# Weights behind the first inputs, first steps on their own, and mixture pieces carried over a block's end

## The chip, the cores and the metric

One core of one Trainium2 chip. The metric is the device time of one execution in microseconds (us), the span of that core. The kernel before has a median of 1416.5 us in three runs. The engines are PE (TensorE matmul), DVE (VectorE), ACT (ScalarE), POOL (GpSimd) and SP (SyncE, which issues most transfers).

## The reference, cut to what matters

An RWKV-7 attention (batch 4, 8 heads, 768 steps, head size 40) feeds a dense mixture of four experts (3072 rows of 320, hidden size 1024).

```python
for t in range(S):                      # attention, per batch and head
    y[:, :, t] = einsum('bhd,bhde->bhe', rt, state)
    Sa = einsum('bhde,bhe->bhd', state, at)
    state = state * wt[:, :, None, :] - einsum('bhd,bhe->bhde', Sa, bt) + einsum('bhd,bhe->bhde', vt, kt)
# ... rows (B*S, H*D) ...
p = domain_probs / (domain_probs.sum(-1, keepdims=True) + 1e-09)
for e in range(E):                      # mixture
    h = np.maximum(x @ w1[e], 0.0)
    out += p[:, e:e + 1] * (h @ w2[e])
```

## The kernel before

The 768 steps are cut into 12 chunks of 64, done in seven blocks: block zero has one chunk, blocks one to five have two each, block six has one. For each block the attention goes through four stages.

- **Units** (two per chunk). Each unit's inputs natW, natNK, natKN, natA, natR are loaded, transposed on PE (pW, pNK, ...), scaled, and multiplied to triangles (pef). The triangles go through HBM (FD) into the tile Gl. There is one tile of each nat kind, so a unit's load waits until the unit before has been transposed.
- **Solve**: one long chain of DVE instructions on Gl, about 30 us.
- The solution goes through HBM to F and XT, and PE works on it (pi, px).
- **Steps**: the recurrence, then a gather into xT for the mixture.

The mixture of block y runs on PE among the attention of block y+1, as a queue of pieces. Each of the four experts has four *wide* pieces (ph: 20 matmuls in a block of two chunks, then a relu on ACT), then four *narrow* ones (po: 16 matmuls, then an *eviction*, which scales po by the gate and writes it to osb; on DVE). `mix(us)` gives out so many us of pieces at that place of the program:

```python
def bank(name):                                    # attention's PSUM banks
    early and early.append(0)
    if len(early) % 2:
        return mbank(name)
    return ps.tile([P, 512], FP32, name=name, tag="bank", bufs=4)

def mbank(name):                                   # the mixture's: four
    return ps.tile([P, 512], FP32, name=name, tag="mbank", bufs=4)

def wide(e, f):
    if f == 0:
        weights(e)                                 # w1s, w2s: one tile each
    ph = [mbank("ph") for _ in range(2)]
    ...
def narrow(e, tt):
    po = mbank("po")
    ...
    if e == 0:
        nc.vector.tensor_scalar(out=osb[tt][:], in0=po[:, 0:DM], scalar1=sc, ...)
    else:
        nc.vector.scalar_tensor_tensor(...)        # osb += sc * po

def mix(us):
    if not queue and ahead:
        stage(*ahead.pop(0))
    credit[0] += us * credit[1]
    while queue and credit[0] >= queue[0][0] / 2:
        t, piece = queue.pop(0)
        credit[0] -= t
        piece()

def attention(b):
    us = b.units
    stage(us[0], 1)
    for y, u in enumerate(us):                     # units
        stage(u, 2)
        if y + 1 < len(us):
            stage(us[y + 1], 1)
        mix(4.3)
        stage(u, 3)
        mix(2.2)
        stage(u, 4)
        ...                                        # FD -> Gl
    ...
    solve(b.n * NP * 4 * M)
    mix(56)
    ...                                            # inverse, steps with mix, gather

for y, b in enumerate(all_blocks):
    credit[:] = [0.0, sum(t for t, _ in queue) / 137]
    attention(b)
    mix(1e9)                                       # flush what is left
    queue += mixture(b.cs, b.xT)
```

Of the kernel before, what the change touches and what calls it, by code (L numbers as in the profile page):

```python
# [14 lines left out]
def kernel(  # L15
# [34 lines left out]
    nc = tc.nc  # L50

    B, H, S, D = r.shape
# [7 lines left out]
    NP = B // 2  # L60
# [20 lines left out]
    def mbank(name):  # L81
        return ps.tile([P, 512], FP32, name=name, tag="mbank", bufs=4)
# [10 lines left out]
        out=ident[:], in_=ident[:], pattern=[[1, P]], compare_op=ALU.is_equal, fill=0.0,  # L93
        base=0, channel_multiplier=-1,
    )
    for x in ("NK", "KN", "A", "R"):
# [10 lines left out]
        out=upper[:], in_=upper[:], pattern=[[1, P]], compare_op=ALU.is_ge, fill=0.0,  # L107
# [6 lines left out]
    RV = [const.tile([P, 2, NJ, 2, 64], FP32, name=f"RV{p}_") for p in range(NP)]  # L114
    VS = [const.tile([P, 2, NJ, 2, 64], FP32, name=f"VS{p}_") for p in range(NP)]
    XT = [const.tile([P, 2, M, L], FP32, name=f"XT{p}_") for p in range(NP)]

    DG = 8 * (Q + 1)
    Xl, Tl, Gl = (const.tile([P, 4 * DG], FP32, name=x) for x in ("Xl", "Tl", "Gl"))

    def clear():
        for t in (Xl, Tl):
            nc.gpsimd.memset(t[:], 0.0)
        for t in (Xl, Tl):
            nc.gpsimd.memset(t[:, 0:Q * Q].rearrange("p (a c) -> p a c", c=Q)[:, 0:1, 0:1], 1.0)
            nc.gpsimd.memset(t[:, Q + 1:Q + 1 + (Q - 1) * (Q + 1)].rearrange("p (a c) -> p a c", c=Q + 1)[:, :, 0:1], 1.0)
        for t in XT + RV + VS:
            nc.gpsimd.memset(t[:], 0.0)


# [3 lines left out]
    def gates():  # L134
        for i in range(2):
            for p in range(NP):
                o = (2 * p + i) * S
                nc.gpsimd.dma_start(
                    out=gate[SL[i]:SL[i] + L, :, p, :], in_=moe_domain_probs[o:o + S, :].rearrange("(c t) e -> t c e", t=L),
                )  # L140
        g = gate[:].rearrange("p c b e -> p (c b) e")
        nc.vector.reduce_sum(out=total[:], in_=g, axis=AX.X)
        nc.vector.tensor_scalar_add(out=total[:], in0=total[:], scalar1=1e-9)
        nc.vector.reciprocal(out=total[:], in_=total[:])
        nc.vector.tensor_mul(g, g, total[:, :, None].to_broadcast([P, NC * NP, E]))

    def half(s):
        return slice(SL[s], SL[s] + 64)
# [4 lines left out]
    def load(x, u):  # L153

        for i in range(2):
            n = nat[x][half(i)]
            src = [y[2 * u.p + i, :, u.t, :] for y in srcs[x]]
            if srcs[x][0] is srcs[x][1]:
                nc.sync.dma_start(out=n[:, :, 0:D], in_=src[0].rearrange("h t e -> t h e"))
                continue  # L160
            for s in range(2):
                nc.sync.dma_start(out=n[:, s::2, 0:D], in_=src[s][s::2].rearrange("h t e -> t h e"))  # L162

    def turn(x):

# [282 lines left out]
    def gather(yD, x, xT):  # L448

        n = B * L  # L450
        for d in range(2):
            nc.sync.dma_start(
                out=xT[half(d), :, x * n:(x + 1) * n],
                in_=yD[:].rearrange("h d b t -> (h d) (b t)").rearrange("(k p) x -> p k x", p=64),
            )

    def mixture(cs, xT):

        n = len(cs) * B * L
        NTT = n // P  # L460
        osb, w = [], {}

        def weights(e):
            w1s = wts.tile([P, NK, F // 2], FP32, name="w1s", tag="w1s", bufs=1)
            w2s = wts.tile([P, NF, DM], FP32, name="w2s", tag="w2s", bufs=1)
            for d in range(2):
                nc.gpsimd.dma_start(  # L467
                    out=w1s[half(d)],
                    in_=moe_w1[e, :, d * (F // 2):(d + 1) * (F // 2)].rearrange("(k p) f -> p k f", p=64),
                )  # L470
            nc.gpsimd.dma_start(out=w2s[:], in_=moe_w2[e].rearrange("(f p) d -> p f d", p=P))  # L471
            w[e] = (w1s, w2s, [])

        def wide(e, f):
            if f == 0:
                weights(e)
            w1s, _, hs = w[e]
            ph = [mbank("ph") for _ in range(2)]
            for k_ in range(NK):
                for d in range(2):  # L480
                    nc.tensor.matmul(  # L481
                        out=ph[d][:, 0:n], lhsT=w1s[half(d), k_, f * P:(f + 1) * P], rhs=xT[half(d), k_, 0:n],
                        start=(k_ == 0), stop=(k_ == NK - 1),
                    )
            for d in range(2):
                hs.append((f + d * NF // 2, mo.tile([P, 2 * B * L], FP32, name="hs", tag="hs", bufs=NF)))
                nc.scalar.activation(out=hs[-1][1][:, 0:n], in_=ph[d][:, 0:n], func=ACTF.Relu)  # L487

        def narrow(e, tt):
            _, w2s, hs = w[e]  # L490
            po = mbank("po")
            for x, (f, h) in enumerate(hs):
                nc.tensor.matmul(  # L493
                    out=po[:, 0:DM], lhsT=h[:, tt * P:(tt + 1) * P], rhs=w2s[:, f, :],
                    start=(x == 0), stop=(x == NF - 1),
                )
            sc = gate[:, cs[tt // NP], tt % NP, e:e + 1]
            if e == 0:
                osb.append(mo.tile([P, DM], FP32, name="osb", tag="osb", bufs=5))
                nc.vector.tensor_scalar(out=osb[tt][:], in0=po[:, 0:DM], scalar1=sc, scalar2=None, op0=ALU.mult)  # L500
            else:
                nc.vector.scalar_tensor_tensor(  # L502
                    out=osb[tt][:], in0=po[:, 0:DM], scalar=sc, in1=osb[tt][:], op0=ALU.mult, op1=ALU.add,
                )
            if e == E - 1:
                for i in range(2):
                    row = (2 * (tt % NP) + i) * S + cs[tt // NP] * L
                    nc.sync.dma_start(out=out[row:row + L, :], in_=osb[tt][half(i)])

        return [piece for e in range(E) for piece in  # L510
                [(n / 119, lambda e=e, f=f: wide(e, f)) for f in range(NF // 2)]
                + [(4.3, lambda e=e, tt=tt: narrow(e, tt)) for tt in range(NTT)]]
# [8 lines left out]
    def stage(u, upto):  # L521

        while u.at < upto:
            u.at += 1
            (decays, scaled, triangles, natural)[u.at - 1](u)

    queue, ahead, credit = [], [], [0.0, 1.0]

    def mix(us):

        if not queue and ahead:
            stage(*ahead.pop(0))
        credit[0] += us * credit[1]
        while queue and credit[0] >= queue[0][0] / 2:
            t, piece = queue.pop(0)
            credit[0] -= t
            piece()

    def attention(b):
        us = b.units  # L540
        stage(us[0], 1)
        for y, u in enumerate(us):
# [7 lines that stand above are left out]
            if u.x == b.n - 1:  # L550
                nc.sync.dma_start(
                    out=Gl[u.q.lanes, 0:Q * Q], in_=u.q.FD[:].rearrange("s z m r t -> (s z m) (r t)"),
                )
        if b.cs[0] == 0:
            clear()
            gates()
        early.clear()
        solve(b.n * NP * 4 * M)
        mix(56)
        for x in range(2):  # L560
            for q in b.qs:
                inverse(q, x)
            mix(4.3)
        if b.cs[0] == 0:
            ahead.extend((u, upto) for u in all_blocks[1].units[0:NP] for upto in range(1, 5))
        b.xT = mo.tile([P, NK, 2 * B * L], FP32, name="xT", tag="xT", bufs=2)
        for x in range(b.n):
            yD = hbm.tile([H, D, B, L], FP32, name="yD", tag="yD", bufs=4)
            steps = [step(u, yD) for u in us[x * NP:(x + 1) * NP]]
            while True:  # L570
                said = [next(y, None) for y in steps]
                if None in said:
                    break
                mix(said[0])
            gather(yD, x, b.xT)

    all_blocks = [block(cs) for cs in [[0]] + [[c, c + 1] for c in range(1, NC - 1, 2)] + [[NC - 1]]]
    early.append(0)
    for y, b in enumerate(all_blocks):
        credit[:] = [0.0, sum(t for t, _ in queue) / 137]  # L580
        attention(b)
        mix(1e9)
        queue += mixture(b.cs, b.xT)
    mix(1e9)


# [26 lines left out]
```

## Time and profile before

| | before |
|---|---|
| median | 1416.5 us |
| span of the profiled run | 1413.4 us |
| PE busy, idle | 1255.5, 157.9 us |
| PE waits for natW | 45.5 us, of it 38.8 at the five starts of blocks two to six |
| PE waits for natW, natA, natKN of units one to three in block three | 3.4 us |
| ph waits for a DVE eviction | 8.8 us |
| from px of block three to px of block five, halved | 215.9 us |

px is a PE operation that each block does once, just after the solve; from one block's px to the next is the pitch of a block in the steady part of the kernel, with nothing of the first and last blocks in it.

### The profile page before, as it was taken

The numbers are of one execution on the slowest core, as the hardware profiler recorded it, in microseconds if no ns is written. First come the engines' busy times: TensorE is split into PE (matmuls) and PEld (weight loads), VectorE is DVE, ScalarE is ACT, GpSimd is POOL, SyncE is SP. The second block draws the span as 40 slices with busy tenths as digits, with TensorE's granted clock in tenths as the row PEclk, the third lists the DMA queues.
The fourth block names the chain that finished last, engine by engine and source line by source line (L and its number), as shares of the span: only waits on it lengthen the run. The fifth ranks groups of instructions, "written<-read, shape, count | busy, mean of one in ns | idle before, by whom it ended". The sixth has DMA issues, their size and how long they took to land.

```text
span 1413.4 us, 26645 instructions
## 1 busy us (share of the span) xinstructions
PE 1255.5 (89%) x11680; PEld 874.3 (62%) x11680; DVE 592.3 (42%) x877; ACT 262.8 (19%) x521; POOL 75.2 (5%) x108
## 2 busy tenths in 40 slices
PE   4167878978999978999978999979899979999998
PEld 4166656856557756557755657656557665566676
DVE  7744572345623345623345443345452335612000
ACT  1021212112121203111203112203113202120111
POOL 3000000000000000000000000000000000000010
PEclk9997988889999989999989999989999999999999
DMA  8233654456353446354445353354462353414363
GB/s 135 44 57 73 115 137 106 82 113 105 91 118 80 90 105 95 82 123 95 85 108 94 81 127 70 91 125 85 93 127 58 85 133 65 93 46 103 93 148 86
DMA packets 284020, 135.75 MB, mean 96 GB/s; under 512 B 246977, under 2 KB 265473, under 8 KB 283905
## 3 DMA queue, kind: packets, MB, share of 16 engines
q1 hardware_dynamic: 266304, 60.60, 24.6%
q0 software_dynamic: 17600, 73.46, 21.1%
q8 instruction: 92, 1.51, 0.5%
q14 instruction: 24, 0.19, 0.0%
HBM read 116.70 MB, written 17.30 MB: 95 GB/s over the span
## 4 chain that ended last, share of the span: by engine, by line
PE 70%; DMA 13%; DVE 10%; SPq 4%; issue 2%; ACT 1%; POOL 0%; DVEq 0%; ACTq 0%
PE ph L481 26%; PE po L493 23%; DVE tmp L288 3%; DMA natW<-in_w_dram 3%; PE pc L418 3%; PE pef L218 3%; DMA natKN<-in_b_dram 2%; DMA natA<-in_a_dram 2%; DMA w1s<-in_moe_w_dram 2%; SPq L162 2%; PE pa L379 2%; PE py L430 2%; PE pt L389 2%; PE py L436 1%; PE pSN L351 1%
## 5 line engine op out<-in xcount | busy, mean ns | idle before, releaser
L481 PE MATMUL ph<-xT,w1s 64*128 64x512 f32 (+1 forms) x2240 | 455.5, 553 | 18.1 <-DVE osb L502 8.1
L493 PE MATMUL po<-w2s,hs 128*128 128x320 f32 x1536 | 430.1, 437 | 0.0
L493 PEld LDWEIGHTS po<-w2s,hs 128*128 128x128 f32 x1536 | 289.4, 191 | 122.6 <-issue 8.5
L481 PEld LDWEIGHTS ph<-xT,w1s 64*128 64x128 f32 x2240 | 226.7, 196 | 210.1 <-issue 182.1
L487 ACT ACTIVATE hs<-ph 128x512 f32<-128x512 f32 (+1 forms) x224 | 110.4, 534 | 623.9 <-PE ph L481 623.0
L502 DVE SCALAR_TENSOR_TENSOR osb<-po,gate,osb 128x320 f32<-128x320 f32 x72 | 39.1, 549 | 370.1 <-PE po L493 370.1
L191 DVE RECIPROCAL GI<-G 128x512 f32<-128x512 f32 x24 | 80.5, 3353 | 0.8
L467 POOL DMA_DIRECT2D w1s<-in_moe_w_dram x56 | 37.8, 679 | 770.2 <-PE ph L481 770.2
L168 PE MATMUL pW<-ident,natW 128*128 128x128 f32 x96 | 18.6, 327 | 50.1 <-DMA natW<-in_w_dram 45.5
L329 PE MATMUL pi<-F 32*32 32x32 f32 x768 | 16.5, 199 | 47.0 <-DMA F<-XD 47.0
L218 PEld LDWEIGHTS pef<-AE,KNT 64*128 64x128 f32 x768 | 50.2, 199 | 12.6 <-issue 11.4
L471 POOL DMA_DIRECT2D w2s<-in_moe_w_dram x28 | 26.0, 928 | 545.7 <-PE po L493 545.7
L288 DVE TENSOR_TENSOR tmp<-Xl,Gl 128x1024 f32<-128x1024 f32 (+5 forms) x49 | 54.2, 1107 | 0.9
L225 DVE TENSOR_TENSOR AE<-pef,mask 64x512 f32<-64x512 f32 x48 | 33.1, 689 | 51.1 <-ACT F L223 50.3
L186 DVE TENSOR_TENSOR_SCAN G<-w_shift,first 128x520 f32<-128x520 f32 x24 | 29.8, 1242 | 56.1 <-ACT w_shift L184 55.9
L218 PE MATMUL pef<-AE,KNT 64*128 64x64 f32 x768 | 51.3, 283 | 2.2 <-DVE AE L205 2.1
L418 PEld LDWEIGHTS pc<-R,VST 64*128 64x128 f32 x768 | 47.8, 199 | 6.8 <-issue 4.2
L418 PE MATMUL pc<-R,VST 64*128 64x64 f32 x768 | 48.9, 284 | 2.0 <-DVE VST L357 1.4
L184 ACT COPY w_shift<-pW 128x512 f32<-128x512 f32 x24 | 14.0, 585 | 192.0 <-PE pW L168 189.5
L329 PEld LDWEIGHTS pi<-F 32*32 32x32 f32 x768 | 15.0, 115 | 52.0 <-issue 44.7
L168 PEld LDWEIGHTS pW<-ident,natW 128*128 128x128 f32 x96 | 13.1, 166 | 54.0 <-issue 48.1
L223 ACT COPY F<-pef 64x512 f32<-64x512 f32 x48 | 27.8, 580 | 99.5 <-PE pef L218 98.9
(104 smaller groups left out, 1013.7 us busy)
## 6 DMA issues: line engine op xcount, KB each, us to landing
w1s<-in_moe_w_dram POOLq DMA_DIRECT2D x56, 640.0 KB, 8.1
w2s<-in_moe_w_dram POOLq DMA_DIRECT2D x28, 1280.0 KB, 7.3
xT<-yD SPq DMA_DIRECT2D x24, 320.0 KB
natW<-in_w_dram SPq DMA_DIRECT2D x48, 80.0 KB
natA<-in_a_dram SPq DMA_DIRECT2D x48, 80.0 KB
natR<-in_r_dram SPq DMA_DIRECT2D x48, 80.0 KB
yD<-Yo SPq DMA_DIRECT2D x48, 80.0 KB
out_dram<-osb SPq DMA_DIRECT2D x48, 80.0 KB
```

Of the source, the lines that this page charges most:

```text
L168: nc.tensor.transpose(out=p[:, j * P:(j + 1) * P], in_=nat[x][:, 2 * j:2 * j + 2, :].rearrange("p h e -> p (h e)"), identity=ident[:],)
L191: nc.vector.reciprocal(out=u.GI[:], in_=u.G[:, :, 1:L + 1])
L218: nc.tensor.matmul(out=pef[s][:, m * L:(m + 1) * L], lhsT=KNT[half(s), m].rearrange("p x t -> p (x t)"), rhs=u.AE[half(s), s, m, :], start ...
L225: nc.vector.tensor_tensor(out=u.AE[o, s], in0=cut(pef[s][o]), in1=mask[o, None, :].to_broadcast([64, M, L]), op=ALU.mult,)
L288: nc.vector.tensor_tensor(out=m, in0=in0[:, :, None, :].to_broadcast([P, n0, n1, nr]), in1=in1[:, None, :, :].to_broadcast([P, n0, n1, nr] ...
L329: nc.tensor.matmul(out=p[hi, at], lhsT=f[lo, m, Q:L], rhs=f[lo, m, 0:Q], start=True, stop=True, tile_position=(SL[s], SL[s] + Q),)
L418: nc.tensor.matmul(out=pc[s][:, m * L:(m + 1) * L], lhsT=VST[half(s), i, j * P:(j + 1) * P], rhs=u.R[half(s), m, :], start=True, stop=True,)
L467: nc.gpsimd.dma_start(out=w1s[half(d)], in_=moe_w1[e, :, d * (F // 2):(d + 1) * (F // 2)].rearrange("(k p) f -> p k f", p=64),)
L481: nc.tensor.matmul(out=ph[d][:, 0:n], lhsT=w1s[half(d), k_, f * P:(f + 1) * P], rhs=xT[half(d), k_, 0:n], start=(k_ == 0), stop=(k_ == NK ...
L487: nc.scalar.activation(out=hs[-1][1][:, 0:n], in_=ph[d][:, 0:n], func=ACTF.Relu)
L493: nc.tensor.matmul(out=po[:, 0:DM], lhsT=h[:, tt * P:(tt + 1) * P], rhs=w2s[:, f, :], start=(x == 0), stop=(x == NF - 1),)
L502: nc.vector.scalar_tensor_tensor(out=osb[tt][:], in0=po[:, 0:DM], scalar=sc, in1=osb[tt][:], op0=ALU.mult, op1=ALU.add,)
```

## The change

It has three parts. Part one lets the first block's inputs come ahead of the weights and lets ACT's queue issue some of them. Part two takes the staging of block one out of block zero's steps; only the decays are done early, ahead of the first solve. Part three keeps up to 13 us of narrow pieces (three of them) at each block's end and gives them out among the next block's units, so that PE has work while the next units' inputs land.

```diff
     def clear():
-        for t in (Xl, Tl):
+        for t in RV + VS + [Xl, Tl]:
             nc.gpsimd.memset(t[:], 0.0)
         ...
-        for t in XT + RV + VS:
+        for t in XT:
             nc.gpsimd.memset(t[:], 0.0)
@@ load
+            by = nc.scalar if u.c == 0 and x in ("KN", "R") else nc.sync
-                nc.sync.dma_start(out=n[:, :, 0:D], ...)
+                by.dma_start(out=n[:, :, 0:D], ...)
@@ weights
+            if cs[0] == e == 0:
+                for t in (w1s, w2s):
+                    nc.gpsimd.tensor_copy(out=t[:, 0, 0:1], in_=all_blocks[0].units[1].KNT[:, 0, 0, 0:1])
@@ mix
-        if not queue and ahead:
-            stage(*ahead.pop(0))
@@ attention
         if b.cs[0] == 0:
             clear()
             gates()
+            for u in after.units[0:NP]:
+                stage(u, 1)
         ...
-        if b.cs[0] == 0:
-            ahead.extend((u, upto) for u in all_blocks[1].units[0:NP] for upto in range(1, 5))
@@ the loop over blocks
-        attention(b)
-        mix(1e9)
+        attention(b, all_blocks[min(y + 1, len(all_blocks) - 1)])
+        credit[:] = [sum(t for t, _ in queue) - 13, 1.0]
+        mix(0)
         queue += mixture(b.cs, b.xT)
-    mix(1e9)
+    credit[0] = 1e9
+    mix(0)
```

More of the change, by code (lines that the diff above doesn't have):

```diff
@@ L157, in load @@
             src = [y[2 * u.p + i, :, u.t, :] for y in srcs[x]]
+            by = nc.scalar if u.c == 0 and x in ("KN", "R") else nc.sync
             if srcs[x][0] is srcs[x][1]:
-                nc.sync.dma_start(out=n[:, :, 0:D], in_=src[0].rearrange("h t e -> t h e"))
+                by.dma_start(out=n[:, :, 0:D], in_=src[0].rearrange("h t e -> t h e"))
                 continue
             for s in range(2):
-                nc.sync.dma_start(out=n[:, s::2, 0:D], in_=src[s][s::2].rearrange("h t e -> t h e"))
+                by.dma_start(out=n[:, s::2, 0:D], in_=src[s][s::2].rearrange("h t e -> t h e"))
     def turn(x):
@@ L525, in stage @@
             (decays, scaled, triangles, natural)[u.at - 1](u)
-    queue, ahead, credit = [], [], [0.0, 1.0]
+    queue, credit = [], [0.0, 1.0]
     def mix(us):
-        if not queue and ahead:
-            stage(*ahead.pop(0))
         credit[0] += us * credit[1]
@@ L537, in mix, with attention @@
             piece()
-    def attention(b):
+    def attention(b, after):
         us = b.units
```

## The prediction

> **What bounds the kernel now.** I read the page first, then its slices, the waits of PE, the timeline around one block's start and around the first block, and the busy times by stretch. One core; the metric is its span, 1413.4 us in the profile (1416.5 us the median time). PE is busy 1255.5 us, so 158 us of the span is PE standing idle, and that is what a change of order can win.
>
> ```profile
> PE 1255.5 (89%) x11680; PEld 874.3 (62%) x11680; DVE 592.3 (42%) x877; ACT 262.8 (19%) x521; POOL 75.2 (5%) x108
> ...
> PE   4167878978999978999978999979899979999998
> ```
>
> The second line (slices of 35 us, PE busy in tenths) shows where: the first four slices, and a dip every six slices, one per block of two chunks. The busy times by stretch put numbers on it: 0 to 125 us has 61.3 us of PE, 330 to 508 has 173.6 of 178. So the middle of a block is bound by PE; the first block and the block starts are bound by something else. The waits of PE name it (total, times, longest):
>
> ```profile
> PE pi L329 <- DMA F<-XD: 47.0, 9, 37.2
> PE pW L168 <- DMA natW<-in_w_dram: 45.5, 10, 8.4
> PE pA L168 <- DMA natA<-in_a_dram: 8.6, 4, 4.2
> ```
>
> The first is the first block's solve (37.2 us with no mixture to hide it). The second is the block starts. The timeline of one start, PE alone, then the queue of SP:
>
> ```profile
> 495.16 13.19 PE L493 MATMUL po<-w2s,hs 128*128 128x320 f32 x48
> 508.19 0.60 PE L168 MATMUL pW<-ident,natW 128*128 128x128 f32 x4
> ...
> 517.89 1.09 PE L168 MATMUL pW<-ident,natW 128*128 128x128 f32 x4 [7.79 <-DMA natW<-in_w_dram]
> ```
>
> ```profile
> 508.82 0.66 SPq L159 DMA_DIRECT2D natW<-in_w_dram  x1
> ...
> 509.52 1.46 SPq L508 DMA_DIRECT2D out_dram<-osb  x2
> ...
> 511.03 0.71 SPq L159 DMA_DIRECT2D natW<-in_w_dram  x1
> ```
>
> Three mixture pieces (48 matmuls) are flushed, only then the first unit's natW is transposed, and only that frees the single natW tile for the second unit's load. That load is issued at 508.82, is split by an output store, and shares the engines with the w2s load that POOL issued at 508.65; it lands about 517.6. PE idles 7.79 us. The five starts show 8.39, 7.79, 7.67, 7.19 and 7.76 us.
>
> In the first block:
>
> ```profile
> 16.59 4.23 SPq L162 DMA_DIRECT2D natKN<-in_b_dram  x1
> ...
> 28.65 1.09 PE L168 MATMUL pNK<-ident,natNK 128*128 128x128 f32 x4 [4.87 <-DMA natNK<-in_k_dram]
> ...
> 43.80 0.16 DVE L272 TENSOR_TENSOR tmp<-Xl,Gl 64x4 f32<-64x4 f32 x1 [5.07 <-DMA Gl<-FD]
> ...
> 92.21 3.34 DVE L191 RECIPROCAL GI<-G 128x512 f32<-128x512 f32 x1
> ...
> 95.47 0.63 DVE L357 COPY SN<-pSN 128x512 f32<-128x512 f32 x1
> ```
>
> Unit 1's inputs, issued from 11.72 us on, are not used before 28.65: the weights (2.6 MB, issued at 12.13) are in their way, and SP's issue itself hangs 4.23 us. The solve starts at 43.80. Later, the next block's reciprocal stands in front of a copy that the first block's step needs.
>
> **What the Trainium skill says.** "DMA: Bandwidth & Descriptors", section "Issuing engines are not separate DMA queues": transfers started by any engine share the same 16 DMA engines; a second issuer saves issue time only. The section "Queues, rings and completion order" has each engine go round its rows packet by packet. The trace agrees: natW loads land some 2.1 us after issue when alone (541.51 issued, PE at 544.92) and 6 us beside w2s. "TensorE: Matmul & The Clock Gate", "Part 1: The HAM clock gate": after an idle window of about 3.4 us PE runs at half rate until it has been busy as long. Agrees: four transposes take 0.60 us before the wait and 1.09 after, and the ph piece behind it 6.64 against 4.56. "GPSIMD Engine Reference", "Specifications": GpSimd shares its SBUF interface with VectorE. Agrees: a 64x64 mask copy took 6.53 us and ended at 9.10 with the last POOL memset; the new order of memsets has the same sum, so G still starts near 9.3.
>
> **Part 1: inputs first.** KN and R of the first block go to ACT's queue: four issues of 0.62 us and one pair of 1.3 per unit leave SP, useful but short. The weights now wait for a one-column POOL copy that reads unit 1's KNT. Step by step with the old durations: unit 0 is bound by mask, G (1.24), GI (3.35) and its products, as before, to 16.4. G and GI of unit 1 end at 21.05. PE is cold: pef 3.7 from 16.5, pkn 1.97, pR 1.06, so unit 1's transposes stand at 23 to 26, KNT at 25, pef from 27.0 instead of 32.70: 5.7 us earlier. The weights then start at about 25.5 and, at the 336 GB/s seen in 24 to 26 us, need 8 us more or less: until about 35. F's store (32 us) is caught by their tail, so I count 3 us of the 5.7: solve from 41 instead of 43.80.
>
> **Part 2: first steps alone.** Before, four stages of two units of block 1 were woven into the steps: on DVE 2 x (1.24 + 3.35 + 1.37 + 1.40 + 1.41) = 17.5 us. Now only decays are done early: 2 x 4.6 us on DVE, one in the wait for Gl, one inside the solve, which so grows by 4.6 (28.8 to 33.4). The steps: pa 3.7, SN 3.7, pt 2.1, VS 0.5, pd 1.5, RV adds 4.0, VST copies 1.3, pc's remainder 3.2, CX 0.7, py 4, Yo 0.7 make 25 instead of 38.6 us (85.1 to 123.7). Gather: about 1 us later, behind four NK issues. Block 0 together: -3 + 4.6 - 13.6 + 1 = -11 us.
>
> The price is in block 1: scaled, triangles and natural of two units now run there, PE 2 x 5.4 us. Some of it falls in the wait for xT (7.45 us) and in other gaps; block 1 is bound by latency (22.2 us PE of 35 in 125 to 160). I count 6 us given back. Net -5.
>
> **Part 3: thirteen us of pieces kept back.** The order on PE shows it: after the last py, pW, pNK, pKN, pA come at once, then the second pW, then one piece, pef, one piece, and so on. natW's second load no longer waits for 13 us of pieces nor queues behind their stores: SP puts it right behind the yD store. With B the end of py: yD issued until B + 1.5, natW until B + 2.8, landed B + 5.3. PE has transposes until B + 2.2, so it waits about 3 us instead of 7.76 (mean). Cold PE: before 0.5 + 2.0 us, now about 1. Per start -4.8 - 1.5 = -6.3; five starts: -31 us. The pieces themselves are the same number; total PE work doesn't change.
>
> What may not go away: w2s of the next expert set now loads after the last kept piece, some 26 us into the block, and meets natA and natW of unit 2. Before, w1s met natA there (3.3 to 4.2 us idle). I count the same.
>
> **Sum.** -5 - 31 = -36; I keep 2 back for new collisions: 1416.5 - 34 = 1382.
>
> **Rivals.** (a) natW's wait is only moved: the load now shares the engines with the yD store and the gather, and lands as late as before. For: weights always make a 2 us load a 6 to 9 us one. Against: w2s is now gated by later pieces, and w1s was issued some 12 us before B. It would leave about -2 per start and 1405. (b) The attention chain becomes the bound: before, F lands at about 626.2 and PE reaches pi at 628.33, only 2 us of slack, and block four already waits 0.5 us. For: w1s now comes just at the unit phase's end and delays F's store and Gl. Against: pieces between the last unit's triangles and pi grow by one (from 13 to 14 pieces of 4.4 us). If it bites, 5 us per block: 1400. (c) Block 1 pays everything back: unit 3's inputs collide with w1s again, 9 us later than before: net +2 in the head, 1389. (d) The head gains in full, F's store isn't caught, and PE stays warm at the starts: 1368.
>
> **Range and chances.** Each start -3 to -8, head +2 to -12: 8 times in 10 between 1366 and 1397. Faster by 2% means below 1388.2; the centre is 6 us under it: 0.66. Within 2%: 0.32. Slower by 2% would need a stall of 12 us per block that nothing shows: 0.02.
>
> **What would show it.** PE's wait for natW near 16 us in total instead of 45.5; first solve operation at 41; its end 2 us later than before; steps of the first block some 25 us, first ph at about 120 instead of 131.25; PE busy slightly down (less cold), the middle of blocks unchanged. Wrong if natW's wait stays over 30 us, if pi waits for F in blocks three to six, or if block 1's pi, 216.7 before, isn't earlier.

## More of the kernel before

The order of each engine's instructions is fixed when the program is built.

In the timeline of PE before, the last px groups of blocks three and five (start, duration, engine, line, operation, shapes, number of matmuls):

```profile
635.93 1.18 PE L334 MATMUL px<-XT__103,F 32*32 32x32 f32 x64
```

```profile
1067.74 1.18 PE L334 MATMUL px<-XT__103,F 32*32 32x32 f32 x64
```

(1067.74 − 635.93) / 2 = 215.9 us.

## The result

The changed kernel takes 1435.09 us (median of four runs, 1433.05 to 1437.01) against 1416.0 us of the kernel before (four runs, 1414.84 to 1416.57). It is slower: the ratio is 1.0136, with a 95% interval of 1.0118 to 1.0153. (A ratio, here and below, is the mean time of one kernel's fast runs over that of the other's of the same rounds, so not quite the ratio of the medians.) That is within the band of 2%, and far outside the predicted range of 1366 to 1397 us.

The page of the changed kernel, its engines:

```profile
PE 1260.6 (88%) x11680; PEld 878.3 (61%) x11680; DVE 592.0 (41%) x877; ACT 262.9 (18%) x521; POOL 75.8 (5%) x110
```

The same 11680 matmuls. Busy time grew by 5.1 us (matmuls at the slow clock), and idle time, span less busy, from 157.9 to 172.1 us. The waits of PE, without the first row (what waits, for what: total us, times, longest):

```profile
PE pW L170 <- DMA natW<-in_w_dram: 43.3, 14, 8.3
PE ph L487 <- DVE osb L508: 16.3, 2, 13.4
PE ph L487 <- DVE osb L506: 15.4, 8, 3.7
PE pA L170 <- DMA natA<-in_a_dram: 9.5, 3, 4.6
```

and of the kernel before, the row that corresponds to line 506:

```profile
PE ph L481 <- DVE osb L500: 0.7, 1, 0.7
```

Two readings. natW is waited for as long as before (43.3 for 45.5 us), in 14 places for 10. This sum mixes two things: up to block one's px all waits for inputs together grew from 13.7 to 21.2 us, and behind it, where the kept pieces act, they fell from 52.4 to 46.4. And ph waits for evictions: 15.4 us for the first expert's (line 506) for 0.7 before, and 16.3 for the others' (8.1 before).

**The start of a block.** Block three, before, is in the prediction: one wait of 7.79 us. Here it is after the change, PE alone:

```profile
493.66 0.66 PE L170 MATMUL pW<-ident,natW 128*128 128x128 f32 x4
...
498.86 0.63 PE L170 MATMUL pW<-ident,natW 128*128 128x128 f32 x4 [3.23 <-DMA natW<-in_w_dram]
499.32 6.16 PE L499 MATMUL po<-w2s,hs 128*128 128x320 f32 x16
...
529.17 1.09 PE L170 MATMUL pA<-ident,natA 128*128 128x128 f32 x4 [4.14 <-DMA natA<-in_a_dram]
533.23 1.09 PE L170 MATMUL pW<-ident,natW 128*128 128x128 f32 x4 [2.97 <-DMA natW<-in_w_dram]
534.25 6.05 PE L487 MATMUL ph<-xT,w1s 64*128 64x512 f32 x20
```

The first wait is 3.23 us, as foreseen (the five starts show 3.17, 3.23, 3.19, 3.59, 3.38). But 30 us later two new waits stand in front of unit two, of 4.14 and 2.97 us, and the ph piece behind them takes 6.05 us where a warm one takes 4.56. (Cold and warm name the clock that the profile shows PE to be granted: 1.00 of full speed from 524 to 526 us, 0.50 from 528 to 534.) What they run into shows in the issues of POOL and of SP:

```profile
520.48 0.93 POOL L477 DMA_DIRECT2D w2s<-in_moe_w_dram  x1 [36.99 <-PE po L499]
```

```profile
521.31 0.60 SPq L161 DMA_DIRECT2D natA<-in_a_dram  x1
522.00 1.22 SPq L514 DMA_DIRECT2D out_dram<-osb  x2
523.28 0.65 SPq L161 DMA_DIRECT2D natA<-in_a_dram  x1
...
529.75 1.31 SPq L161 DMA_DIRECT2D natW<-in_w_dram  x2
```

The next w2s (1.28 MB) may only load when the last kept piece has read the old one, at 520.48, and natA is issued 0.8 us later. The chain of waits has natA landing at 528.31, 7.0 us after its first issue, and the 16 DMA engines are full from 524 to 528 us (a share of 1.00, then 1.12); natW is issued only behind that, at 529.75. That w2s is what holds natA up is read from this order and not tested by a run; an output store also stands between natA's two halves (522.00). All waits of PE for inputs in block three, added up: before 7.79 + 0.50 + 2.92 = 11.2 us, after 3.23 + 0.70 + 4.14 + 2.97 = 11.0 us. In block four, 11.8 and 11.9. With three pieces kept the wait was moved, not removed.

**The solve.** Block three, PE, before:

```profile
562.70 5.16 PE L493 MATMUL po<-w2s,hs 128*128 128x320 f32 x16
...
571.68 8.78 PE L493 MATMUL po<-w2s,hs 128*128 128x320 f32 x32
580.39 17.44 PE L481 MATMUL ph<-xT,w1s 64*128 64x512 f32 x80
597.76 17.50 PE L493 MATMUL po<-w2s,hs 128*128 128x320 f32 x64
```

and after:

```profile
561.02 17.39 PE L499 MATMUL po<-w2s,hs 128*128 128x320 f32 x64
578.34 1.12 PE L487 MATMUL ph<-xT,w1s 64*128 64x512 f32 x2
580.23 4.56 PE L487 MATMUL ph<-xT,w1s 64*128 64x512 f32 x18 [0.77 <-DVE osb L506]
585.05 1.12 PE L487 MATMUL ph<-xT,w1s 64*128 64x512 f32 x2 [0.27 <-DVE osb L506]
589.84 15.84 PE L487 MATMUL ph<-xT,w1s 64*128 64x512 f32 x58 [3.67 <-DVE osb L506]
605.62 17.49 PE L499 MATMUL po<-w2s,hs 128*128 128x320 f32 x64
```

Before, the first two of the four narrow pieces of expert one are done among the units, and the four wide ones of expert two take 17.4 us (580.39 to 597.76). After, the three kept pieces have taken the room among the units, all four narrow pieces come in one run, and the same four wide ones take from 578.34 to 605.62, 27.3 us: 9.9 us more. DVE at the same time, after the change:

```profile
565.73 0.17 DVE L274 TENSOR_TENSOR tmp<-Xl,Gl 128x4 f32<-128x4 f32 x1 [8.31 <-DMA Gl<-FD]
...
572.79 0.54 DVE L506 TENSOR_SCALAR osb<-po,gate 128x320 f32<-128x320 f32 x1
...
579.64 0.53 DVE L506 TENSOR_SCALAR osb<-po,gate 128x320 f32<-128x320 f32 x1
...
584.46 0.54 DVE L506 TENSOR_SCALAR osb<-po,gate 128x320 f32<-128x320 f32 x1
...
589.24 0.55 DVE L506 TENSOR_SCALAR osb<-po,gate 128x320 f32<-128x320 f32 x1
```

The solve begins at 565.73, and the four evictions of half a microsecond each stand at fixed places between its instructions. The last po ends at 578.4; its eviction runs at 589.24, and at 589.84 PE goes on. The mixture has four PSUM banks: four narrow pieces fill them, and ph, which needs two, gets each bank only when the solve's order lets an eviction through. The last wait, 3.67 us, also leaves PE cold: the granted clock is 0.50 from 590 to 594 us, and 58 matmuls of ph take 15.84 us, where 60 took 13.14 in the kernel before (at 615.18). Each restart of PE (580.23, 585.05, 589.84) comes within 0.1 us of the end of an eviction. Blocks four and five look alike: waits of 3.67 and 3.68 us, then 58 matmuls in 15.09 and 14.84. The same stretch of four wide pieces is 7.2 us longer than before in block four, 7.2 in block five and 3.0 in block six: with block three some 27 us.

**The head.** It also came out behind. The first solve begins at 42.73 (43.80 before), the steps run from 88.70 to about 112.6 and the first ph is at 121.22 (131.25 before), ten us ahead. But block one's px is at 232.25 (224.77 before). Its units now hold all the work that was staged early except the decays, and its solve starts late. POOL, SP and DVE, before:

```profile
173.41 0.93 POOL L471 DMA_DIRECT2D w2s<-in_moe_w_dram  x1 [24.94 <-PE po L493]
```

```profile
171.56 0.49 SPq L551 DMA_DIRECT2D Gl<-FD  x1
```

```profile
174.99 0.17 DVE L272 TENSOR_TENSOR tmp<-Xl,Gl 128x4 f32<-128x4 f32 x1 [1.28 <-DMA Gl<-FD]
```

and after:

```profile
172.24 0.93 POOL L477 DMA_DIRECT2D w2s<-in_moe_w_dram  x1 [17.57 <-PE po L499]
```

```profile
174.15 0.47 SPq L555 DMA_DIRECT2D Gl<-FD  x1
```

```profile
182.45 0.17 DVE L274 TENSOR_TENSOR tmp<-Xl,Gl 128x4 f32<-128x4 f32 x1 [9.92 <-DMA natR<-in_r_dram]
```

Before, Gl is issued 1.9 us ahead of w2s and the solve starts 3.4 us later. After, w2s is 1.9 us ahead, and the solve starts 8.3 us after Gl's issue. The view puts this last wait down to natR, which SP issues just behind Gl, though the instruction reads Gl and not natR. In "Flush all" below, whose program is the same up to there, the same wait is put down to Gl:

```profile
182.49 0.17 DVE L274 TENSOR_TENSOR tmp<-Xl,Gl 128x4 f32<-128x4 f32 x1 [9.40 <-DMA Gl<-FD]
```

### The profile page after: what moved, and what is told of

Same layout as the page of the kernel before. It is cut to its first block, busy times and chain, and to the rows that moved or that the text cites. A ratio compares the mean times of both kernels' runs of the same rounds, so it can differ in the third digit from the quotient of the medians.

```text
span 1432.7 us, 26662 instructions
## 1 busy us (share of the span) xinstructions
PE 1260.6 (88%) x11680; PEld 878.3 (61%) x11680; DVE 592.0 (41%) x877; ACT 262.9 (18%) x521; POOL 75.8 (5%) x110
## 4 chain that ended last, share of the span: by engine, by line
PE 69%; DVE 13%; DMA 11%; SPq 4%; issue 2%; ACT 0%; POOL 0%; DVEq 0%
PE ph L487 26%; PE po L499 21%; DVE tmp L290 5%; PE pc L420 3%; PE pef L220 2%; DVE Y L294 2%; DMA FD<-F 2%; DMA natW<-in_w_dram 2%; PE py L432 2%; PE pa L381 2%; PE pt L391 2%; PE pSN L353 2%; PE py L438 2%; DMA natA<-in_a_dram 2%; SPq L164 2%
## 5 line engine op out<-in xcount | busy, mean ns | idle before, releaser
L487 PE MATMUL ph<-xT,w1s 64*128 64x512 f32 (+1 forms) x2240 | 462.5, 555 | 40.9 <-DVE osb L508 16.3
L487 PEld LDWEIGHTS ph<-xT,w1s 64*128 64x128 f32 x2240 | 232.3, 196 | 234.4 <-issue 177.1
L359 DVE COPY SN<-pSN 128x512 f32<-128x512 f32 x24 | 16.6, 692 | 118.2 <-PE pSN L353 118.2
L170 PE MATMUL pW<-ident,natW 128*128 128x128 f32 x96 | 18.5, 325 | 46.8 <-DMA natW<-in_w_dram 43.3
L331 PE MATMUL pi<-F 32*32 32x32 f32 x768 | 16.3, 199 | 48.3 <-DMA F<-XD 48.3
L227 DVE TENSOR_TENSOR AE<-pef,mask 64x512 f32<-64x512 f32 x48 | 33.1, 689 | 55.1 <-ACT F L225 54.3
L426 DVE TENSOR_TENSOR CX<-pc,mask 128x512 f32<-128x512 f32 x48 | 30.9, 686 | 34.1 <-PE pc L420 34.1
```

What stands on the lines that cost most here:

```text
L170: nc.tensor.transpose(out=p[:, j * P:(j + 1) * P], in_=nat[x][:, 2 * j:2 * j + 2, :].rearrange("p h e -> p (h e)"), identity=ident[:],)
L227: nc.vector.tensor_tensor(out=u.AE[o, s], in0=cut(pef[s][o]), in1=mask[o, None, :].to_broadcast([64, M, L]), op=ALU.mult,)
L331: nc.tensor.matmul(out=p[hi, at], lhsT=f[lo, m, Q:L], rhs=f[lo, m, 0:Q], start=True, stop=True, tile_position=(SL[s], SL[s] + Q),)
L487: nc.tensor.matmul(out=ph[d][:, 0:n], lhsT=w1s[half(d), k_, f * P:(f + 1) * P], rhs=xT[half(d), k_, 0:n], start=(k_ == 0), stop=(k_ == NK ...
```

## The experiments

Two theories. **S**: the loss comes from the three kept pieces, by pushing the first expert's narrow pieces into the solve, where their evictions wait in DVE's order; the head (parts one and two) loses a little as well. **H**, the rival: the kept pieces gain as predicted, and the loss is all in the head. All twelve runs gave correct results. Each edit is shown against the kernel named.

### Flush all

The changed kernel without part three.

```diff
-        credit[:] = [sum(t for t, _ in queue) - 13, 1.0]
+        credit[0] = 1e9
```

> The changed kernel with all pieces flushed before the next block, as the kernel before does it: parts 1 and 2 alone. Theory S (the three kept pieces push the first expert's narrow pieces into the solve, where their evictions stand in DVE's queue behind it and PE runs out of PSUM banks): what is left is the head's own loss, 7.6 us at px of block one, and blocks three to six take the 215 us they took before: about 1424. PE's waits for osb in blocks three to five vanish, its waits for natW at the five starts are back at 7 to 8 us. Theory H (the loss is all in the head and carried along, the kept pieces are a gain): 1424 + 25 = about 1450.

Measured: 1421.53 us (1421.0 to 1423.02), ratio 1.0056 (1.0037 to 1.0075). The waits for the first expert's evictions are back to 0.7 us. So parts one and two cost some 7 us by themselves (the kernel before had 1414.27), and part three some 14 us on top. H falls.

### Keep three, nothing else

The kernel before with part three alone.

```diff
-        mix(1e9)
+        credit[:] = [sum(t for t, _ in queue) - 13, 1.0]
+        mix(0)
```

> The kernel before with only part 3: thirteen us of pieces kept back. Theory S: block two gains 9 us (one kept piece), blocks three, four and five lose 9, 7 and 6 as in the changed kernel: about 1416 - 9 + 22 = 1429, with PE waiting for osb some 4 us per block. Theory H: the starts gain as predicted, about 1385.

Measured: 1429.55 us (1425.7 to 1431.97), ratio 1.0108 (1.0084 to 1.0133). ph waits 13.6 us for the first expert's evictions. Part three costs 15 us without the other two, 14 with them.

### Keep one

The changed kernel with 4.3 us kept, one narrow piece.

```diff
-        credit[:] = [sum(t for t, _ in queue) - 13, 1.0]
+        credit[:] = [sum(t for t, _ in queue) - 4.3, 1.0]
```

> The changed kernel with 4.3 us (one piece) kept back in place of 13. Block two of the changed kernel had just one kept piece and gained 9 us. Theory S: every block from two to five then gains some 8 us against before, the head loses 7.6: about 1395, no wait for osb in blocks three to five, natW waits of 3 us at the starts. If instead the loss comes from the weights meeting the units' inputs whenever anything is kept: 1425 or more.

Measured: 1399.34 us (1395.39 to 1402.7), ratio 0.9905 (0.9878 to 0.9932): 36 us less than with three kept, by one number. ph waits 2.1 us for the first expert's evictions, and for natW PE waits 33.1 us for 43.3. Keeping pieces is a gain as long as it is one.

### Evictions on ACT

The changed kernel, three pieces kept, with the first expert's evictions on ACT, which has no part in the solve.

```diff
-                nc.vector.tensor_scalar(out=osb[tt][:], in0=po[:, 0:DM], scalar1=sc, scalar2=None, op0=ALU.mult)
+                nc.scalar.activation(out=osb[tt][:], in_=po[:, 0:DM], func=ACTF.Copy, scale=sc)
```

> The changed kernel with the first expert's narrow pieces evicted by ACT (a scaled copy) in place of DVE, so that they no longer queue behind the solve. Theory S: the 15.4 us that PE waits for osb of the first expert vanish, and the cold matmuls behind them (some 2 us in each of three blocks): about 1435 - 20 = 1415. If the lost time of blocks three to five is in the unit phase instead (natA, natW and the cold clock behind them), under 5 us change: 1430 or more.

Measured: 1408.11 us (1406.0 to 1410.93), ratio 0.996 (0.9937 to 0.9984). It is the direct test of S: order, number and place of the pieces are those of the changed kernel, only the engine that empties the banks is another, and 27 us are gone. S had foreseen 20. In the profiled runs PE's idle time falls by 17.9 us (172.1 to 154.2) and its busy time by 10.5 (1260.6 to 1250.1), so the cold matmuls behind the waits cost more than the 6 us reckoned. PE in block three:

```profile
563.55 17.39 PE L499 MATMUL po<-w2s,hs 128*128 128x320 f32 x64
580.87 17.44 PE L487 MATMUL ph<-xT,w1s 64*128 64x512 f32 x80
```

and ACT at the end of the last of the four narrow pieces:

```profile
580.98 0.53 ACT L506 ACTIVATE osb<-po,gate 128x320 f32<-128x320 f32 x1 [3.78 <-PE po L499]
```

The four narrow pieces are still one run of 64 matmuls, but each is emptied as soon as it ends, and the wide ones behind them take 17.44 us again for 27.3. The Trainium skill has this on its page "Perfetto Trace Analysis", section "Matmuls": independent groups should rotate through PSUM banks so that their evacuation by ACT or DVE overlaps the next matmuls. This trace agrees. The changed kernel adds that the overlap ends where the evacuating engine's order holds something long in front: the same stretch is 9.9 us longer there.

### Inputs first alone

The kernel before with part one alone. Its copy that gates the weights reads a small tile filled from unit one's KNT, because with the old staging KNT itself is overwritten first.

```diff
+            nc.gpsimd.tensor_copy(out=mark[:], in_=us[1].KNT[:, 0, 0, 0:1])   # behind clear() and gates()
...
-                    nc.gpsimd.tensor_copy(out=t[:, 0, 0:1], in_=all_blocks[0].units[1].KNT[:, 0, 0, 0:1])
+                    nc.gpsimd.tensor_copy(out=t[:, 0, 0:1], in_=mark[:])
```

> The kernel before with the first part alone: memsets reordered, the first two loads by a second queue, the weights behind the first block's inputs; the staging of block one inside the first steps is put back and the pieces are flushed as before. Parts one and two together cost 7.5 us (1421.5). Theory H1 (that cost is part two's: block one's units must now do work that used to be hidden in the first steps): 1413, between 1410 and 1416, first op of the solve at 42 to 43 instead of 43.8. Rival H2 (the cost is part one's: the weights are loaded at worse moments and hold up the rows of the solve in block one): 1421, between 1418 and 1425.

Measured: 1413.67 us (1411.18 to 1415.55), ratio 0.9999 (0.9973 to 1.0025). Nothing. Block zero's last px group begins at 82.85 for 83.80, one us earlier, and block one's at 227.25 for 224.77.

### First steps alone

The kernel before with part two alone.

```diff
+            for u in all_blocks[1].units[0:NP]:
+                stage(u, 1)
...
-        if b.cs[0] == 0:
-            ahead.extend((u, upto) for u in all_blocks[1].units[0:NP] for upto in range(1, 5))
```

> The kernel before with the second part alone: only the decays of block one's first two units are staged ahead of the first solve, the first steps stand alone. H1: 1423, between 1419 and 1427, with block one's px some 8 us later than before (224.8 becomes 231 to 234). H2: 1414, between 1411 and 1417.

Measured: 1422.56 us (1421.06 to 1424.15), ratio 1.0062 (1.0041 to 1.0082), block one's px at 236.27, which is later than the 231 to 234 expected. The cost of the head is part two's.

### Keep one, with the old staging

Inputs first and one piece kept; part two undone.

```diff
-        credit[:] = [sum(t for t, _ in queue) - 13, 1.0]
+        credit[:] = [sum(t for t, _ in queue) - 4.3, 1.0]
+            ... (ahead as before, mark as two runs above)
```

> Inputs first, the staging inside the first steps put back, and one narrow piece kept at each block's end instead of three. The kernel with one piece kept and the first steps alone took 1399.3. H1: 8 us less, 1391, between 1388 and 1395, block one's px near 225. H2: no gain over it, 1399, between 1397 and 1402.

Measured: 1390.75 us (1386.08 to 1396.52), ratio 0.9838 (0.9805 to 0.9872), block one's px at 226.63. The two findings add up: faster than both kernels by 1.6% and 3%.

### Keep one, old staging, evictions on ACT

The edit of "Evictions on ACT", on the kernel of the run before.

```diff
-                nc.vector.tensor_scalar(out=osb[tt][:], in0=po[:, 0:DM], scalar1=sc, scalar2=None, op0=ALU.mult)
+                nc.scalar.activation(out=osb[tt][:], in_=po[:, 0:DM], func=ACTF.Copy, scale=sc)
```

> The kernel of the run before this one, with the first expert's evictions moved from VectorE to ScalarE. With one piece kept, the waits of ph for those evictions were only 2.1 us in all, so the theory that the evictions stand in VectorE's solve gives little here: 2 us less than its neighbour, 1389, between 1385 and 1392. If moving the evictions helped by lightening VectorE anywhere (not only in the solve), it would gain 10 or more: 1380.

Measured: 1391.49 us (1386.27 to 1392.52), ratio 0.9834 (0.9809 to 0.986), the same as its neighbour. So moving the evictions is no gain by itself; it paid 27 us only where they stood in the solve. This closes a way out for S, that ACT is merely the less loaded engine.

### w2s behind Gl

The kernel "Keep one" (with the first steps alone), and block one's second w2s waits for Gl.

```diff
+            if cs[0] == 0 and e == 1:
+                nc.gpsimd.tensor_copy(out=w2s[:, 0, 0:1], in_=Gl[:, 0:1])
             nc.gpsimd.dma_start(out=w2s[:], in_=moe_w2[e].rearrange("(f p) d -> p f d", p=P))
```

> The kernel with one piece kept and the first steps alone (1399.3), and in block one the second expert's w2s waits for the rows of the solve (a GpSimd copy of one column from Gl into w2s ahead of its load). There the w2s load was issued 2 us ahead of the last Gl load and the solve of block one started at 181.6. Theory: w2s and Gl collide, and half of what the first steps alone cost is this: the solve starts at 177 to 179, px of block one near 229 instead of 232.8, 1395 in all, between 1392 and 1398. Rival: the late start is only the late last unit, the order of the two loads moves nothing: solve at 181 or later and 1399 or more.

Measured: 1390.96 us (1386.65 to 1396.21), ratio 0.9846 (0.9814 to 0.9877). SP's issue of Gl and DVE's start of the solve:

```profile
173.37 0.48 SPq L557 DMA_DIRECT2D Gl<-FD  x1
```

```profile
177.03 0.17 DVE L274 TENSOR_TENSOR tmp<-Xl,Gl 128x4 f32<-128x4 f32 x1 [4.87 <-DMA Gl<-FD]
```

3.7 us from issue to solve, for 7.8 in "Keep one" with w2s ahead; the solve starts at 177.03 for 181.56, and px of block one comes at 227.39 for 232.76. So the collision is a real part of part two's price, up to there. In the whole time the gain was larger than expected, 8 us where 4 were foreseen. The two kernels' intervals only just part, the runs of each differ by 7 to 10 us among themselves, and the two profiled runs are equal at px of block five (1050.66 and 1050.77), so there the 5 us have been lost again. I take 5 us in block one as shown and leave the rest open.

### Keep two

The kernel "Keep one, with the old staging", with 8.6 us kept.

```diff
-        credit[:] = [sum(t for t, _ in queue) - 4.3, 1.0]
+        credit[:] = [sum(t for t, _ in queue) - 8.6, 1.0]
```

> The kernel with inputs first, staging inside the first steps and one piece kept (1390.8), with two pieces kept instead of one. Theory S: the second kept piece pushes the last of the first expert's four narrow pieces behind the start of the solve, where their evictions stand between VectorE's own instructions: ph waits for the first expert's osb 6 to 12 us in all (2.2 with one piece kept, 15.4 with three in the changed kernel), 1405, between 1398 and 1412. Rival (more pieces in the starts are simply better until they run out): 1385, between 1380 and 1389.

Measured: 1405.42 us (1401.49 to 1411.38), ratio 0.9952 (0.9914 to 0.9991). ph waits 11.3 us for the first expert's evictions, inside the 6 to 12 expected. And natW is waited for less than with one piece kept, 21.8 us for 26.1: the second piece does fill more of the starts, and loses more in the solve than it fills.

### Keep one, nothing else

The kernel before with one line changed.

```diff
-        mix(1e9)
+        credit[:] = [sum(t for t, _ in queue) - 4.3, 1.0]
+        mix(0)
```

> The kernel before with one line changed: one narrow piece kept at each block's end, nothing else. Inputs first gave nothing by itself (1413.7), so this should equal its neighbour with it: 1391, between 1387 and 1395. Rival: inputs first pays once the starts are filled: 1394 to 1398 here.

Measured: 1389.38 us (1385.69 to 1395.5), ratio 0.9837 (0.9805 to 0.987). The lowest median, level with "Keep one, with the old staging", which has part one besides. Its waits of PE:

```profile
PE pW L168 <- DMA natW<-in_w_dram: 24.9, 9, 4.1
PE pR L168 <- DMA natR<-in_r_dram: 8.5, 4, 2.6
PE ph L481 <- DVE osb L502: 8.0, 2, 5.1
...
PE ph L481 <- DVE osb L500: 3.0, 3, 1.3
PE pA L168 <- DMA natA<-in_a_dram: 2.5, 3, 1.1
```

natW has fallen by 20.6 us and natA by 6.1; natR, for which PE did not wait before, takes 8.5, and the first expert's evictions cost 2.3 more. All rows together, the small ones too, fall by 23.4 us (153.3 to 129.9), which is the size of the 24 us gained. (PE's busy time is 4 us higher in this profile, and its run, 1395.5 us, is the slowest of the four.) In block three PE waits 7.0 us for inputs for 11.2 before: 3.78 at the start, 1.94 at unit two and 1.31 for natR.

### Keep three at the old rate

The rate of `mix` counts the kept pieces too, so with three of them it is (137 + 13) / 137 = 1.1, and more pieces come ahead of pi. The changed kernel with the kept ones left out of the rate:

```diff
-        credit[:] = [0.0, sum(t for t, _ in queue) / 137]
+        credit[:] = [0.0, (sum(t for t, _ in queue) - 13 * (y > 1)) / 137]
```

> The changed kernel as it is, but the rate at which pieces are given out in a block counts only that block's own pieces, so it is 1.0 as before and not 1.1 with the three kept ones. Rival R (the loss of three pieces comes from the higher rate, which puts more pieces ahead of pi): 1410, between 1400 and 1420. Theory S (the loss comes from the first expert's evictions in VectorE's solve): they move still deeper into the solve, 1438, between 1430 and 1448, ph's waits for them 15 us or more.

Measured: 1450.83 us (1449.58 to 1454.67), ratio 1.0272 (1.0248 to 1.0296). The higher rate was no cause of the loss; without it the loss is larger. But the time lies above all that S foresaw (1430 to 1448). The waits for the first expert's evictions are 15.9 us, as S says, but barely more than the 15.4 of the changed kernel, so the 16 us that this kernel loses further are not in them. The px of the two profiled runs, 20.3 us apart, show where they fall: 9.2 us from block one's px to block two's (196.3 for 187.1), 3.1 from block five's to block six's, and 8.3 behind the last px (172.4 for 164.0), with nothing in blocks three to five. natW's wait has grown from 43.3 to 50.5, which is less than half of it; the cause I have not traced.

### All of them

| kernel | pieces kept | first steps | evictions of expert one | median us | pitch of blocks three to five | ph waits for expert one's evictions, in all |
|---|---|---|---|---|---|---|
| before | 0 | staged | DVE | 1416.0 | 215.9 | 0.7 |
| inputs first alone | 0 | staged | DVE | 1413.67 | 214.0 | 0.7 |
| first steps alone | 0 | alone | DVE | 1422.56 | 214.8 | 0.7 |
| flush all | 0 | alone | DVE | 1421.53 | 215.3 | 0.7 |
| keep one, nothing else | 1 | staged | DVE | 1389.38 | 211.1 | 3.0 |
| keep one, old staging | 1 | staged | DVE | 1390.75 | 209.0 | 2.2 |
| the same, ACT | 1 | staged | ACT | 1391.49 | 210.2 | none |
| keep one | 1 | alone | DVE | 1399.34 | 209.6 | 2.1 |
| w2s behind Gl | 1 | alone | DVE | 1390.96 | 210.4 | 2.2 |
| keep two | 2 | staged | DVE | 1405.42 | 215.0 | 11.3 |
| keep three, nothing else | 3 | staged | DVE | 1429.55 | 221.9 | 13.6 |
| the change | 3 | alone | DVE | 1435.09 | 222.3 | 15.4 |
| keep three at the old rate | 3 | alone | DVE | 1450.83 | 222.3 | 15.9 |
| evictions on ACT | 3 | alone | ACT | 1408.11 | 214.6 | none |

The kernel before is the first comparison's; later its median was 1414.27, 1414.25 and 1413.59. The pitch is from one profiled run each, worked out as above. It goes by the number of pieces kept and by the engine of the evictions, and hardly by anything else: some 215 us with none, 209 to 211 with one, 215 with two, 222 with three, and 215 with three when ACT evicts.

## Why the prediction was wrong

**The inputs ahead of the weights** (−3 us in the sum): the step was mis-sized. Up to F's store it went as foreseen: the weights were issued at 25.08, the store by 31.3. But the solve began at 42.73, not 41, since the store was caught by the weights more than I had allowed: in the chain of waits after the change FD takes 9.46 us to land, until 40.30. I had let the weights pass at 336 GB/s until about 35; the DMA engines were full (0.96 to 1.08) from 24 to 40 us, and all transfers together made 171 to 269 GB/s. Alone, this part moved nothing.

**The first steps alone** (−11 in block zero, 6 given back): the half in block zero was right (10.0 us at the first ph). The time from the start of the solve to pi grew from 33.25 to 38.0 us, 4.8 for a predicted 4.6; the steps took 24 us for 25; the first ph came at 121.22 for 120. The half in block one failed. "I count 6 us given back" should have been about 17.5: from the first ph to the solve of block one went from 131.25 to 174.99 before and from 121.22 to 182.45 after. Some 5 us of it are the collision of w2s with Gl that "w2s behind Gl" took away; the other 12 I put down to the units' own work and waits, which no run took apart; "Keep one" against "w2s behind Gl" shows the 5 us only up to block one. Rival (c) had a collision too, of unit three's inputs with w1s, and priced the head at +2; it came as +7.5 at block one's px, and the transfers were w2s and Gl.

**The kept pieces** (−31): the mechanism at the start was right and its size too. natW's wait there is 3.2 to 3.6 us, predicted 3. Two steps beside it failed. The runs give each a size: with the evictions taken out of the solve ("Evictions on ACT" against "Flush all") the three pieces gain 13 us, 18 short of 31, and the evictions turn these 13 into a loss of 14.

- "w2s of the next expert set now loads after the last kept piece … and meets natA and natW of unit 2 … I count the same." It is not the same: unit two's waits took back all that the start had won (11.2 us of input waits before, 11.0 after, in block three; and with ACT evicting, the pitch is 214.6 us for the 215.3 of "Flush all"). That w2s is the cause of these waits is read from the trace; no run moved it alone. Rival (a), "natW's wait is only moved", was this, with the wrong place. With one piece kept w2s is issued 13.8 us after the block's first pW in block three, not 26.8; unit two then waits 1.94 us for natW and not at all for natA, and 24 of the 31 us are there.
- "The pieces themselves are the same number; total PE work doesn't change", and with it "the middle of blocks unchanged". The number is the same, but the order is turned by three pieces against the solve. The first expert's four narrow pieces fell into the solve all together, filled the four banks of the mixture, and PE stood or ran cold for 9.9, 7.2, 7.2 and 3.0 us in blocks three to six, some 27 us, as much as moving the evictions to ACT won back. I had asked which work lies ahead of PE in the start, not what the pieces need of the other engines at the place where they now end up. Of the rivals none was this one.

The sum, redone from the runs that have one part alone: inputs first nothing (1413.67 for 1414.25), first steps +8 (1422.56), the kept pieces +15 (1429.55 for 1414.27). That makes +23, where the three at once measured +19 in their own comparison. So the parts add up to within a few us, and the miss is the head (some +7 instead of −5) and the kept pieces (+14 or +15 instead of −31).

One reading of the prediction was wrong without consequence: in rival (b), 626.2 us is the end of the issue of F's last load, not its landing, so the 2 us of slack were not shown. Likewise the 2.1 and 6 us of natW's loads count from the end of the issue (542.78 and 511.74).

**What stays open**: whether w2s or something else near it holds up unit two's inputs; the cause of the 16 us more of "keep three at the old rate", and what "w2s behind Gl" won past 5 us. And ph's wait for the later experts' evictions doubled in all kernels with the first steps alone (16 for 8 us), except with w2s behind Gl (6.7 us); it lies in the head and is part of its +7, but I made no run for it alone.

## What to carry to other kernels

When filler work is shifted in time, write down for each piece what it needs of the *other* engines, and look at what those engines have in their order at the new place: an eviction of half a microsecond, placed deep in a 30 us chain, held its PSUM bank for 10.8 us here. Look at such a knob as a dose. One piece kept won 24 us, two won 8, three lost 15, and the first runs should have been those three. And when work is removed from the front of a kernel, follow it to the next point where something must wait for a load, and read who else loads there.

## What the Trainium skill lacked or had wrong

- "Perfetto Trace Analysis", section "Matmuls", has the rotation through PSUM banks, but not that the evictions' place in the evicting engine's own order decides whether it works. (That VectorE's queue keeps its order, the skill says elsewhere; what it means for the rotation, no page says.) Here DVE was busy for 41% of the span and yet held PE up, with the cold stretch behind, by 9.9 us in block three with four evictions of 0.54 us; moving them to ACT won 27 us in all, and nothing (1391.49 for 1390.75 us) where ph hardly waited for them.
- "TensorE: Matmul & The Clock Gate", "Part 1: The HAM clock gate", has PE cold after an idle window of about 3.4 us, and says that this window runs freely, so that its place differs from run to run. With that a wait of 3.23 us can leave PE warm, as in block three of the changed kernel (four transposes in 0.63 us, and only the po piece behind them slow, 6.16 us for 4.58). What doesn't fit is that shorter waits were followed by the cold rate too: four transposes took 1.09 us after a wait of 2.92 us in block three of the kernel before, though they took 0.60 just ahead of it.
- "DMA: Bandwidth & Descriptors", section "Issuing engines are not separate DMA queues", says that transfers interleave, but gives no size for a small one beside a large one: Gl reached the solve 3.4 us after its issue when w2s came behind it, 8.3 us when w2s was issued 1.9 us ahead.
